# Gated attention plus gated FFN: gate ratios turned on TensorE, results finished block by block, spread factors on ScalarE's queue

## The chip, the cores and the metric

The kernel runs on one core of one Trainium2 chip. The metric is the device time of one execution in microseconds; the time before is the median of three runs. Smaller is better. All arithmetic is in float32; where a matmul needs the accuracy, a number is split into a high and a low part and three matmuls replace one.

## The reference

One sequence x of 2048 tokens with 640 features goes through two branches, and a gate per token mixes them:

```python
g = sigmoid((x * gate_w).sum(-1, keepdims=True))
a = attention(x, wq, wk, wv, wo, beta)   # 32 heads of 20, four chunks of 512 tokens
b = (silu(x @ w1) * (x @ w3)) @ w2       # 640 -> 1728 -> 640
out = g * a + (1 - g) * b
```

The attention works on chunks of 512 tokens. In each chunk a causal softmax attention inside the chunk is mixed, by a factor per head, with a read from a memory: `phi(q) @ M / phi(q) @ z`, where M and z are the sums over all earlier chunks of `phi(k)^T v` and `phi(k)`.

The kernel computes the result as `(1 - g) * (b + e * a)` with `e = g / (1 - g)`. The numbers `1 - g` and `e` per token are called here the gate's ratios. `e` is multiplied into the attention's own factors, so that the attention's projection can be added straight to the FFN's sums; `1 - g` scales each result at the very end.

## The kernel before

Everything is kept with features on the partitions and 512 tokens of a chunk along the row, so that a result block is 128 x 512 and a chunk has five (KB). Weights come from DRAM in tiles of 128 x 640 (`wr`, two raw buffers), are split by ScalarE (high part, L104) and GpSimd (low part, L105) into six buffers `W`, and are asked for ahead of their use by `w_step`, which counts steps of the program.

The four chunks are done in two pairs, A = (0, 1) and B = (2, 3). For each pair: projections v, k, q (`v_blocks` L341, `k_block` L380, `q_block` L304), then the FFN in five groups of inner blocks (`ffn_up` L465, `ffn_down` L500, whose sums live in a slot `acc` per chunk), the normalisation of the attention's result (`normalize` L684) and its projection by wo (`oproj` L761), which is added to the same `acc`. The attention runs in quads of four heads (32 quads): scores s (L567) for the row maxima (DVE, L574), the maxima turned and written beside the queries (mr, a DMA of ScalarE's queue, L588), scores again turned (t, L600), exponentials by ScalarE (P, L606), the causal cut by GpSimd (L610), and P times v (o, L620).

TensorE's order is written out by hand: the generator `attention` gives the attention's places, and `step` with a credit in nanoseconds puts the matmuls of the projections and the FFN between them; `braid(a, b, n, skip)` takes one place of job b after every n places of job a, from place `skip` on. The lists of jobs (L858 to L904) are the segments of the program. The orders of all other engines come from a scheduler with its own estimates of durations, except where `here` keeps an instruction at its place. Each engine executes its own list strictly in order, DMA issues included: a DMA that waits holds what is behind it on the issuing engine. DMAs are issued by SP (most), GpSimd (queries and keys of the attention, the weights for k, results of chunks 0 and 1) and ScalarE (mr, v and the gate's ratios).

The buffers that matter here: the tag `acc` has two slots, taken in turn by raw x, V, the FFN sums of a chunk and pq3; the tag `spread` has two buffers (rb and sh); eight PSUM banks go round by `bank_tile` (L109), each filled by TensorE and freed by the engine that reads it.

The pieces that the change touches:

- **Gate.** `v_blocks` gets the gate's sum as one more column of v, ScalarE takes its exponential per token block (L371), DVE makes the two ratios (L375 to L377) in `gate[:, c]`, tokens on the partitions, and L378 stores them to DRAM (`ed`) from there: 128 x 8 single elements, on ScalarE's queue, four steps later.
- **Factors.** When a chunk's quads are done, `o_sums` reads the softmax sums rs and the ratios er, `o_scale` (L656) forms one factor per head and token and writes it to DRAM spread over the 20 rows of a head (`rd`, four DMAs on SP, L661). `normalize` reads it back in five blocks of 128 rows (`rb`, SP, L693), two ahead; L694 and L695 issue the first two, `load(b + 2)` ahead of the yield the others. Each block multiplies `oall`, adds the transposed memory read for chunks 1 to 3 (gt, L706), and is split again.
- **Result.** `load_share` (L669) reads `1 - g` spread over 128 rows (`sh`, SP, L671). For chunks 2 and 3 the last `ffn_down` adds, multiplies (GpSimd for even blocks, DVE for odd) and stores on SP (L523 to L530). For chunks 0 and 1 a job `store(c)` (L789) does it later, braided into other work: five products on GpSimd (L794), five stores on GpSimd's queue (L795).

Of the kernel before, what the change touches and what calls it, by code (L numbers as in the profile page):

```python
# [38 lines left out]
def gated_mix(ctx: ExitStack, tc: tile.TileContext, xT, wqk, wv, w13, w2, w2h, wo, beta, out):  # L39
# [20 lines left out]
    cR = cp.tile([P, 1], F32, name="cR")  # L60
    rs = cp.tile([P, P], F32, name="rs")
    er = cp.tile([P, P], F32, name="er")
    nsT = [cp.tile([P, 32], FR, name=f"ns{i}") for i in range(2)]
    gate = cp.tile([P, NSEG, 2, 4], F32, name="gate")
    Ms = {}
# [275 lines left out]
    def v_blocks(c, iv, end):  # L341
        x = Xs[c]
        keep = c < NSEG - 1
        if keep:
            V = slot(f"V{c}").rearrange("p (l h e) -> p l h e", l=4, e=VE)
            big["v", c] = V
            nc.gpsimd.memset(V[:, :, :, DH:], 1.0)
        wvt = [w_get(i, iv[0]) for i in iv]
        for lb in range(4):
            if keep:  # L350
                vv = V[:, lb]
            else:
                vv = ht_tile([P, H, VE], F32, f"vv{c}_{lb}")
                nc.gpsimd.memset(vv[:, :, DH:], 1.0)
            for hf in range(2):
                n0, n1 = (0, 320) if hf == 0 else (320, 642)
                ps = bank_tile(f"v{c}_{lb}_{hf}", 800)
                n = 0
                for kb in range(KB):
                    for a, b in PASSES:  # L360
                        nc.tensor.matmul(ps[:, :n1 - n0], x[:, a, kb, lb * P:(lb + 1) * P],  # L361
                                         wvt[kb][:, b, n0:n1], start=n == 0, stop=n == 14)
                        n += 1
                    if end and (lb, hf) == (3, 1):
                        clock["oldest"] = iv[kb] + 1
                    if kb in (1, 3):
                        yield 890
                filled()
                last["act"] = nc.scalar.copy(vv[:, 16 * hf:16 * hf + 16, :DH], ps[:, :320].rearrange("p (h e) -> p h e", e=DH))
                if hf == 1:  # L370
                    nc.scalar.activation(gate[:, c, 1, lb:lb + 1], ps[:, 320:321], AF.Exp)  # L371
                yield 450
            store_later(vd[c][:, lb], vv.rearrange("p h e -> p (h e)"), ("v", c, lb), nc.scalar)
        e, g = gate[:, c, 1], gate[:, c, 0]
        nc.vector.tensor_scalar(e, e, TOP, None, op0=ALU.min)  # L375
        nc.vector.tensor_scalar(g, e, 1.0, None, op0=ALU.add)
        nc.vector.reciprocal(g, g)  # L377
        store_later(ed[c].rearrange("x a p -> p (x a)"), gate[:, c].rearrange("p x a -> p (x a)"), ("e", c), nc.scalar)  # L378

    def k_block(c, mb, i, prev):  # L380

        if prev:
            yield from memory_turn(*prev)
        ps = bank_tile(f"k{c}_{mb}", 1300)
        for n, y in enumerate(proj(ps, w_get(i), Xs[c])):
            yield y
            if n == 3 and prev:
                yield from memory_write(*prev)
        pk = None
        if c < NSEG - 1:  # L390
            big["k", c, mb] = pk = f_tile(f"pk{c}_{mb}")
        s = parts(f"ks{c}_{mb}", ps, pk)
        store_parts(1, c, mb, s)
        yield 699
# [102 lines left out]
                nc.vector.tensor_sub(ht[64:, 0], t[:64], ht[:64, 0].bitcast(F32))  # L497
            yield 699

    def ffn_down(cs, js, idx, last=False):  # L500
        first = js[0] == 0
        w2s = [w_get(i, idx[0]) for i in idx]
        for c in cs:
            if first:
                accs[c] = slot(f"acc{c}")[:, :KB * L].rearrange("p (b n) -> p b n", b=KB)
            if last:
                load_share(c)
            for fb in range(KB):
                ps = bank_tile(f"f{c}_{js[0]}_{fb}", 1300 if len(js) > 2 else 690)
                ms = []  # L510
                for j, w in zip(js, w2s):
                    for a, b in (PASSES if j < NF else ((0, 0), (0, 1))):
                        ms.append((w[:, b, fb * P:(fb + 1) * P], hts[c, j][:, a, :]))
                for n, (w, h) in enumerate(ms):
                    nc.tensor.matmul(ps, w, h, start=n == 0, stop=n == len(ms) - 1)  # L515
                    if n % 3 == 2 and n < len(ms) - 1:
                        yield 699.0 if n == 2 else 699
                filled()
                dst = accs[c][:, fb]
                if first:  # L520
                    nc.scalar.copy(dst, ps)  # L521
                elif not last:
                    nc.vector.tensor_add(dst, ps, dst)  # L523
                else:
                    end = (c, fb) == (cs[-1], KB - 1)
                    for n0 in ((0, 256) if end else (0,)):
                        d, p, g = (t[:, n0:n0 + (256 if end else L)] for t in (dst, ps, shares[c]))
                        nc.vector.tensor_add(d, p, d)
                        (nc.vector if end or fb % 2 else nc.gpsimd).tensor_mul(d, d, g)
                        nc.sync.dma_start(out[c, fb, :, n0:n0 + d.shape[-1]], d)  # L530
                yield 699 if len(ms) % 3 == 0 else 466

    oall, heads, pairs = {}, {}, {}
# [122 lines left out]
    def o_scale(c):  # L656

        here(nc.vector.reciprocal(rs, rs))
        nc.vector.scalar_tensor_tensor(rs, rs, cR, er, op0=ALU.mult, op1=ALU.mult)
        for a in range(4):  # L660
            here(nc.sync.dma_start(rd[c][:, :, a * P:(a + 1) * P], rs[a::4].unsqueeze(1).broadcast_to([H, DH, P])))  # L661
        turned.append(c)

    shares = {}
# [3 lines left out]

    def load_share(c):  # L669
        shares[c] = spread(f"sh{c}")  # L670
        here(nc.sync.dma_start(shares[c], ed[c][0].rearrange("a n -> (a n)").unsqueeze(0).broadcast_to([P, L])))  # L671

    gms = {}

# [9 lines left out]
    def normalize(c):  # L684

        rows = rd[c].rearrange("h e n -> (h e) n")
        rb = {}

        def load(b):
            if b < KB:  # L690
                assert c in turned
                rb[b] = spread(f"rb{c}_{b}")
                here(nc.sync.dma_start(rb[b], rows[b * P:(b + 1) * P]))  # L693

        load(0)  # L695
        load(1)
        yield 1
        if not c:
            gms[c] = big_tile(f"oT{c}", FR)[:, :KB * L].rearrange("p (b n) -> p b n", b=KB)
        for b in range(KB):  # L700
            o, hi = rb[b], gms[c][:, b]
            nc.vector.tensor_mul(o, oall[c][:, b].bitcast(F32), o)
            if c:
                pt = bank_tile(f"gt{c}_{b}")
                for qb in range(4):
                    nc.tensor.transpose(pt[:, qb * P:(qb + 1) * P], hi[:, qb * P:(qb + 1) * P].bitcast(F32), ident)  # L706
                nc.vector.tensor_add(o, o, pt)
            nc.scalar.copy(hi, o)
            nc.vector.tensor_sub(oall[c][:, b], o, hi.bitcast(F32))
            load(b + 2)  # L710
            yield 450 if c else 1

    NJ = NSEG * H

# [46 lines left out]
    def oproj(c, plan):  # L761
# [6 lines left out]

        def rest():
            ws.extend(w_get(i, plan[0]) for i in plan)  # L770
            for fb in range(KB):
                ps = bank_tile(f"op{c}_{fb}", 1300)
                n = 0
# [7 lines left out]
                        yield 699  # L781
                filled()
                dst = accs[c][:, fb]
                nc.vector.tensor_add(dst, ps, dst)
                yield 699

        return first(), rest()

    def store(c):  # L789
        load_share(c)  # L790
        yield 1
        for fb in range(KB):
            d = accs[c][:, fb]
            nc.gpsimd.tensor_mul(d, d, shares[c])  # L794
            here(nc.gpsimd.dma_start(out[c, fb], d))  # L795
            yield 1


    GROUPS = [[0, 1, 2], [3, 4, 5], [6, 7, 8], [9, 10, 11], [13, 12]]

# [5 lines left out]
        return [[((2 if j < NF else 1) * 3.5, ffn_up((c,), j, p, plans[0][0])) for j, p in zip(GROUPS[g], plans)]  # L806
                for c in cs]

    def job_down(cs, g, last=False):
        return 2.32 * sum(3 if j < NF else 2 for j in GROUPS[g]), ffn_down(cs, GROUPS[g], plan_down(GROUPS[g]), last)  # L810

    def jobs_up(cs, g):
# [62 lines left out]
    u0, u1 = jobs_up_by_chunk(A, 4)  # L875
    x2, x3 = split_x(2), split_x(3)
    seg += [(0, load_raw(2)), (0, load_raw(3))] + u0 + [braid(chain(u1), (0, x2), 4, 0, False)]
    d = job_down(A, 4)
    q = job_q(B[:1], 0, {2: big_tile})
    seg += [braid(chain([braid(braid(d, (0, store(0)), 2, 8), (0, x2), 5)] + q), (0, x3), 4, 10)] + job_v(B)  # L880
    kb_, turns, writes = jobs_k(B)
    seg += kb_ + turns[:1] + job_q(B[1:], 0, {3: slot}) + turns[1:] + writes
    segs.append((2 * H - 2, seg))
# [7 lines left out]
    segs.append((2 * H + LAG + 2, seg))  # L891
    up.append(job_up(B, 2))
    o1, o2 = jobs_oproj(1)
    seg = [braid(chain(up[1:]), o1, 4, 11), braid(o2, job_read(3), 3, 1), braid(job_down(B, 0), (0, store(1)), 3, 2), braid(chain(jobs_up(B, 1)), (0, load_memory(2)), 5)]
    segs.append((3 * H + LAG + 1, seg))
    d = job_down(B, 1)
    u = [job_up(B, j) for j in GROUPS[2][:2]]
# [3 lines left out]
    segs.append((NJ + LAG, seg))  # L901
    d, u = job_down(B, 3), jobs_up(B, 4)
    o1, o2 = jobs_oproj(3)
    tail = [braid(chain([d] + u), o1, 2, 8)] + [o2, job_down(B, 4, True)]  # L904

    for n, (_, g) in enumerate(head):
        for _ in g:
# [112 lines left out]
```

## Time and profile before

| | us |
|---|---|
| median of 3 runs | 1163.38 (1162.63 to 1166.82) |
| the profiled execution | 1161.55 |
| its span, first to last instruction | 1159.6 |
| TensorE busy (matmuls) | 1104.2 (95%) |
| DVE busy | 582.0 (50%) |
| GpSimd busy | 505.1 (44%) |
| ScalarE busy | 460.4 (40%) |
| mean granted clock of TensorE | 0.979 |

The trace gives each instruction with its start and length in microseconds from the span's start, its engine (PE is TensorE, PEld its weight loads, DVE VectorE, ACT ScalarE, POOL GpSimd, SP SyncE; a q behind the name is a DMA issue of that engine), the line of the kernel, the operation with output and input tiles, and in brackets the idle time of the engine just before and what ended it. A group of like instructions near each other is one row with a count (x15), whose length reaches from the first start to the last end. In the views by windows, each engine has its busy time and in brackets its instructions; then come the granted clock, the share of the 16 DMA engines' time that was busy (packets in flight overlap, so it can pass 1), and GB/s.

### The profile page before, as it was taken

Reading aid. Unit: us, or ns where it says so; the run is one execution under the profiler, and the core shown is the slowest. Engines: PE = TensorE matmul, PEld = TensorE weight load, DVE = VectorE, ACT = ScalarE, POOL = GpSimd, SP = SyncE. Lnnn points to the kernel's source line nnn. Section 1 sums busy time; section 2 is a strip of 40 time slices with the busy share of each in tenths; the row PEclk is TensorE's granted clock in tenths of the full one; section 3 lists DMA queues with packets and bytes.
Section 4 is the critical chain, followed back from the end, with each engine's and each line's share of the span. In section 5 each row is a group of like instructions: output and inputs, shape, how many; then the busy total and the mean of one; then the engine's idle time right before and its main releaser. Section 6 shows DMA issues by size and latency. Waiting matters only on the chain. (4 is left out here: it accounts for less than half of the span.)

```text
span 1159.6 us, 17915 instructions
## 1 busy us (share of the span) xinstructions
PE 1104.2 (95%) x6261; PEld 860.8 (74%) x6261; DVE 582.0 (50%) x1685; ACT 460.4 (40%) x948; POOL 505.1 (44%) x615
## 2 busy tenths in 40 slices
PE   9979999999999999998799997996999889999997
PEld 6968877777777777777677775774777667777785
DVE  5022474355555544474234675772556565561454
ACT  5245334444343324264345543442544343334130
POOL 4044445355354336264254444344654444454143
PEclk8989999999999999999999998998999999999999
DMA  8475853335354426326886868444565444432422
GB/s 300 97 151 209 275 145 90 90 84 131 78 137 122 124 72 181 106 70 195 93 261 205 295 189 202 109 126 120 150 156 146 108 101 107 116 105 85 127 75 99
DMA packets 102648, 163.28 MB, mean 141 GB/s; under 512 B 14560, under 2 KB 38368, under 8 KB 102560
## 3 DMA queue, kind: packets, MB, share of 16 engines
q1 hardware_dynamic: 73760, 114.81, 33.2%
q0 software_dynamic: 21184, 41.30, 15.9%
q10 hardware_dynamic: 7616, 6.05, 2.9%
q8 instruction: 49, 0.80, 0.3%
q14 instruction: 39, 0.32, 0.1%
HBM read 101.80 MB, written 59.79 MB: 139 GB/s over the span
## 5 line engine op out<-in xcount | busy, mean ns | idle before, releaser
L105 POOL TENSOR_TENSOR W<-wr,W 128x640 fp32r<-128x640 f32 (+1 forms) x126 | 197.2, 1571 | 298.1 <-ACT W L104 268.3
L574 DVE CUSTOM_DVE_ANT_0 junk<-s,mask 128x256 bf16<-128x256 f32 (+3 forms) x512 | 250.2, 489 | 118.2 <-PE s L567 85.7
L606 ACT ACTIVATE P<-t 128x512 f32<-128x512 f32 (+1 forms) x384 | 171.9, 536 | 143.6 <-PE t L600 117.0
L250 PE MATMUL g<-X,W 128*128 128x512 f32 x840 | 211.2, 401 | 4.3 <-DVE m L574 3.3
L515 PE MATMUL f<-ht,W 128*128 128x512 f32 x820 | 197.3, 398 | 0.0
L250 PE MATMUL u<-X,W 128*128 128x512 f32 x780 | 195.5, 398 | 0.4 <-DVE m L574 0.4
L250 PEld LDWEIGHTS g<-X,W 128*128 128x128 f32 x840 | 157.4, 190 | 42.0 <-DVE m L574 3.8
L515 PEld LDWEIGHTS f<-ht,W 128*128 128x128 f32 x820 | 153.4, 189 | 36.5
L610 POOL TENSOR_SCALAR_AFFINE_SELECT P<-P 128x256 f32<-128x256 f32 x192 | 93.8, 500 | 176.4 <-ACT P L606 175.8
L250 PEld LDWEIGHTS u<-X,W 128*128 128x128 f32 x780 | 144.1, 188 | 35.1 <-DVE m L574 0.6
L104 ACT CAST W<-wr 128x640 fp32r<-128x640 f32 (+1 forms) x133 | 95.7, 728 | 141.1 <-PE u L250 22.3
L105 POOL TENSOR_TENSOR ht<-ft,ht 128x512 fp32r<-128x512 f32 x52 | 67.3, 1294 | 101.7 <-ACT ht L104 98.6
L620 PE MATMUL o<-P,vg 128*32 128x512 f32 (+3 forms) x1024 | 79.4, 452 | 12.3 <-ACT acc L521 9.0
L544 POOL DMA_DIRECT2D qk<-qkd x128 | 83.1, 651 | 12.8 <-PE t L600 12.7
L250 PE MATMUL k<-X,W 128*128 128x512 f32 x300 | 78.6, 410 | 6.9 <-ACT P L606 6.9
L567 PE MATMUL s<-qk 60*128 60x256 f32 (+3 forms) x512 | 77.8, 346 | 4.0 <-DVE ft L489 1.7
L250 PE MATMUL q<-X,W 128*128 128x512 f32 x300 | 76.7, 410 | 1.5 <-ACT W L104 1.0
L361 PE MATMUL v<-W,X 128*128 128x320 f32 (+1 forms) x480 | 72.3, 311 | 4.1 <-POOL W L105 2.6
L361 PEld LDWEIGHTS v<-W,X 128*128 128x128 f32 x480 | 71.1, 189 | 5.1 <-POOL W L105 3.2
L620 PEld LDWEIGHTS o<-P,vg 128*32 128x32 f32 x1024 | 31.2, 113 | 56.5 <-issue 34.6
L523 DVE TENSOR_TENSOR acc<-f,acc 128x512 f32<-128x512 f32 x70 | 48.0, 689 | 47.5 <-PE f L515 47.4
L250 PEld LDWEIGHTS q<-X,W 128*128 128x128 f32 x300 | 57.3, 194 | 17.6 <-ACT W L104 1.5
(105 smaller groups left out, 1122.1 us busy)
## 6 DMA issues: line engine op xcount, KB each, us to landing
qk<-qkd POOLq DMA_DIRECT2D x128, 240.0 KB, 4.5
wr<-in_w_dram SPq DMA_DIRECT2D x80, 320.0 KB
qkd<-qs SPq DMA_DIRECT2D x20, 512.0 KB
qkd<-ks SPq DMA_DIRECT2D x20, 512.0 KB
od<-oq SPq DMA_DIRECT2D x32, 256.0 KB
wr<-in_wo_dram SPq DMA_DIRECT2D x20, 320.0 KB
vg<-vd SPq DMA_DIRECT2D x16, 336.0 KB
xr<-in_xT_dram SPq DMA_DIRECT2D x20, 256.0 KB
```

What stands on the lines that cost most here:

```text
L104: pin(nc.scalar.copy(dst[:, 0], src))
L105: (lo or nc.gpsimd.tensor_sub)(dst[:, 1], src, dst[:, 0].bitcast(F32))
L250: nc.tensor.matmul(ps, w[:, a, kb * P:(kb + 1) * P], x[:, b, kb, :], start=n == 0, stop=n == 14)
L361: nc.tensor.matmul(ps[:, :n1 - n0], x[:, a, kb, lb * P:(lb + 1) * P], wvt[kb][:, b, n0:n1], start=n == 0, stop=n == 14)
L515: nc.tensor.matmul(ps, w, h, start=n == 0, stop=n == len(ms) - 1)
L523: nc.vector.tensor_add(dst, ps, dst)
L544: here(nc.gpsimd.dma_start(t[64 * i:64 * i + RH], qkd[c][RH * (h + i):RH * (h + i + 1)]))
L567: nc.tensor.matmul(ps[i][:, o:o + w], q[:, qb * P:(qb + 1) * P], key[:, :w], start=n == 0, stop=n == len(todo) - 1, skip_group_check=True)
L574: nc.vector.tensor_tensor_reduce(out=junk[:, :w], in0=ps[i][:, o:o + w], in1=mask[:, L - w:], scale=1.0, scalar=-3.0e38, op0=ALU.add, op1= ...
L606: last["exp"] = nc.scalar.activation(pairs[2 * m + k]["P"][:, i, o:o + n], ps[i][:, b:b + n], AF.Exp, scale=SCALE)
L610: nc.gpsimd.affine_select(d, d, pattern=[[0, 2], [0, n], [1, P]], base=0, channel_multiplier=-1, compare_op=ALU.is_ge, fill=0.0)
L620: nc.tensor.matmul(ps[32 * i:32 * i + 32, kb * P:], heads[2 * p + i]["v"][:, kb], pairs[p + i // 2]["P"][:, i % 2, o:o + n], start=kb == 0 ...
```

## The change

Three things are done.

1. The ratios of a chunk are turned on TensorE: in the first k block of the chunk, after three of its yields (nine matmuls), `gate_turn` transposes `gate[:, c]` (128 x 8) to 8 x 128 in a PSUM bank, ScalarE copies it to one tile `et`, and SP stores it four steps later as eight rows of 512 bytes. The store of L378 goes.
2. `store(c)` and its two jobs go. A helper `finish` adds, multiplies and stores a block at its last sum, for all chunks: chunk 0 in the last `ffn_down` of pair A, chunk 1 in its projection, chunks 2 and 3 in the last `ffn_down` of pair B. Chunks 0 and 1 are stored on SP two steps later, chunks 2 and 3 at once.
3. The DMAs of rd, rb and sh are issued by ScalarE in place of SP, and `load(b + 2)` moves behind the yield of `normalize`.

With the jobs `store(0)` and `store(1)` their braids go too, so the splits of x for chunk 3 (x3) are woven into a shorter list of places; and in the tail the normalisation of chunk 3 is woven one place in five from the tenth on, where it was one in two from the eighth.

```diff
-        store_later(ed[c].rearrange("x a p -> p (x a)"), gate[:, c].rearrange("p x a -> p (x a)"), ("e", c), nc.scalar)
+
+    def gate_turn(c):
+        ps = bank_tile(f"ge{c}")
+        nc.tensor.transpose(ps[:8, :P], gate[:, c].rearrange("p x a -> p (x a)"), ident)
+        nc.scalar.copy(et, ps[:8, :P])
+        store_later(ed[c].rearrange("x a p -> (x a) p"), et, ("e", c))
...
         for n, y in enumerate(proj(ps, w_get(i), Xs[c])):
             yield y
+            if n == 2 and mb == 0:
+                gate_turn(c)
...
-    def ffn_down(cs, js, idx, last=False):
+    def finish(c, fb, ps, end=False):
+        dst = accs[c][:, fb]
+        for n0 in ((0, 256) if end else (0,)):
+            d, p, g = (t[:, n0:n0 + (256 if end else L)] for t in (dst, ps, shares[c]))
+            nc.vector.tensor_add(d, p, d)
+            (nc.vector if end or fb % 2 else nc.gpsimd).tensor_mul(d, d, g)
+            if c < 2:
+                store_later(out[c, fb], d, n=2)
+            else:
+                nc.sync.dma_start(out[c, fb, :, n0:n0 + d.shape[-1]], d)
+
+    def ffn_down(cs, js, idx, last=()):
...
         for c in cs:
+            if c in last:
+                load_share(c)
...
-            if last:
-                load_share(c)
...
-                elif not last:
+                elif c not in last:
                     nc.vector.tensor_add(dst, ps, dst)
                 else:
-                    end = (c, fb) == (cs[-1], KB - 1)
-                    for n0 in ((0, 256) if end else (0,)):
-                        d, p, g = (t[:, n0:n0 + (256 if end else L)] for t in (dst, ps, shares[c]))
-                        nc.vector.tensor_add(d, p, d)
-                        (nc.vector if end or fb % 2 else nc.gpsimd).tensor_mul(d, d, g)
-                        nc.sync.dma_start(out[c, fb, :, n0:n0 + d.shape[-1]], d)
+                    finish(c, fb, ps, (c, fb) == (NSEG - 1, KB - 1))
...
-            here(nc.sync.dma_start(rd[c][:, :, a * P:(a + 1) * P], rs[a::4].unsqueeze(1).broadcast_to([H, DH, P])))
+            here(nc.scalar.dma_start(rd[c][:, :, a * P:(a + 1) * P], rs[a::4].unsqueeze(1).broadcast_to([H, DH, P])))
...
-        here(nc.sync.dma_start(shares[c], ed[c][0].rearrange("a n -> (a n)").unsqueeze(0).broadcast_to([P, L])))
+        here(nc.scalar.dma_start(shares[c], ed[c][0].rearrange("a n -> (a n)").unsqueeze(0).broadcast_to([P, L])))
...
-                here(nc.sync.dma_start(rb[b], rows[b * P:(b + 1) * P]))
+                here(nc.scalar.dma_start(rb[b], rows[b * P:(b + 1) * P]))
...
-            load(b + 2)
             yield 450 if c else 1
+            load(b + 2)
...
         def rest():
             ws.extend(w_get(i, plan[0]) for i in plan)
+            if c == 1:
+                load_share(c)
...
-                nc.vector.tensor_add(dst, ps, dst)
+                if c == 1:
+                    finish(c, fb, ps)
+                else:
+                    nc.vector.tensor_add(dst, ps, dst)
                 yield 699
...
-    def store(c):
-        load_share(c)
-        yield 1
-        for fb in range(KB):
-            d = accs[c][:, fb]
-            nc.gpsimd.tensor_mul(d, d, shares[c])
-            here(nc.gpsimd.dma_start(out[c, fb], d))
-            yield 1
...
-    d = job_down(A, 4)
+    d = job_down(A, 4, (0,))
     q = job_q(B[:1], 0, {2: big_tile})
-    seg += [braid(chain([braid(braid(d, (0, store(0)), 2, 8), (0, x2), 5)] + q), (0, x3), 4, 10)] + job_v(B)
+    seg += [braid(chain([braid(d, (0, x2), 5)] + q), (0, x3), 4, 10)] + job_v(B)
...
-    seg = [braid(chain(up[1:]), o1, 4, 11), braid(o2, job_read(3), 3, 1), braid(job_down(B, 0), (0, store(1)), 3, 2), braid(chain(jobs_up(B, 1)), (0, load_memory(2)), 5)]
+    seg = [braid(chain(up[1:]), o1, 4, 11), braid(o2, job_read(3), 3, 1), job_down(B, 0), braid(chain(jobs_up(B, 1)), (0, load_memory(2)), 5)]
...
-    tail = [braid(chain([d] + u), o1, 2, 8)] + [o2, job_down(B, 4, True)]
+    tail = [braid(chain([d] + u), o1, 5, 10)] + [o2, job_down(B, 4, B)]
```

More of the change, by code (lines that the diff above doesn't have):

```diff
@@ L62, in gated_mix @@
     er = cp.tile([P, P], F32, name="er")
+    et = cp.tile([8, P], F32, name="et")
     nsT = [cp.tile([P, 32], FR, name=f"ns{i}") for i in range(2)]
@@ L709, in normalize @@
             nc.vector.tensor_sub(oall[c][:, b], o, hi.bitcast(F32))
+            yield 450 if c else 1
             load(b + 2)
-            yield 450 if c else 1
     NJ = NSEG * H
@@ L807, in jobs_up_by_chunk, with job_down @@
                 for c in cs]
-    def job_down(cs, g, last=False):
+    def job_down(cs, g, last=()):
         return 2.32 * sum(3 if j < NF else 2 for j in GROUPS[g]), ffn_down(cs, GROUPS[g], plan_down(GROUPS[g]), last)
```

## Prediction

> **What bounds the kernel now.** I read the table of engines first, then the table of TensorE's waits, then the time line around each long wait.
>
> ```profile
> PE   9979999999999999998799997996999889999997
> ```
> ```profile
> PE o L620 <- ACT acc L521: 9.0, 1, 9.0
> PE k L250 <- ACT P L606: 6.9, 1, 6.9
> PE pm L417 <- ACT pkn L404: 6.2, 1, 6.2
> ...
> PE v L361 <- POOL W L105: 2.6, 2, 1.4
> ```
>
> The first row gives TensorE's busy tenths in 40 slices of 29 us: nearly all are 9, so TensorE sets the time, and the end can move only where it waits, where its clock is low, or behind its last matmul. The second fence (releaser: us in total, times, longest) names the places. Its first three waits are 22 us together. The change leaves TensorE's own order as it is but for four small transposes and later turns in the tail, so I go from wait to wait and ask which of its three parts reaches it.
>
> **The change part by part.** The sum is made against the profiled execution: 1161.55 us, a span of 1159.6 and 1.95 around it, 1.8 below the median of 1163.38.
>
> **Part 1, the gate's ratios as rows.** Before, each store of the ratios is 128 x 8 elements of 4 bytes. Two of the four stand ahead of a stall.
>
> ```profile
> 62.34 1.09 POOL L161 DMA_DIRECT2D wr<-in_wqk_dram  x2
> 62.71 0.38 ACTq L269 DMA_DIRECT2D ed<-gate  x1
> 74.33 0.72 ACT L104 CAST W<-wr 128x640 fp32r<-128x640 f32 x1 [4.03 <-DMA wr<-in_wqk_dram]
> 76.56 2.33 PE L417 MATMUL pm<-V,pkn 128*128 128x147 f32 x8 [6.19 <-ACT pkn L404]
> 82.97 1.16 PE L417 MATMUL pm<-V,pkn 128*128 128x147 f32 x8
> ```
> ```profile
> DMA to landing us min/median/max: 3.3/5.2/11.4
> ```
> ```profile
> 550.00:560.00 10.00, 10.00 (x70) 10.00 (x69) 0.00 (x0) 2.28 (x7) 0.00 (x0) 1.00 0.84 68
> ```
> ```profile
> q1 hardware_dynamic: 73760, 114.81, 33.2%
> ```
>
> A time-line row is start, length, engine, line, operation, and in brackets the idle time and what ended it. Two weight loads (wr) and one ratio store (ed) leave together at 62.3 to 62.9. The second load is cast only at 74.33, 11.4 us after its issue, which is the longest landing of all weight loads where the median is 5.2. ScalarE stands in line at that cast, the copy pkn comes behind it, and TensorE waits 6.19 us. The window 550 to 560, where the third such store is in flight, has the DMA engines 84% taken at only 68 GB/s: many tiny pieces. That is 8.4 us of all 16 engines. SP's queue (q1) moved 114.81 MB in 33.2% of the span, 298 GB/s, so 0.68 MB are some 2.3 us of it, and I estimate 6 us for one ratio store. Without it I let the second load land 6.2 us after issue, one over the median: cast at 69.1 in place of 74.33, and the stall shrinks by 5.2. The eight pm matmuls took 2.33 in place of 1.16 at low clock, so 1.2 more: **6.4**. Bounds: 0 (the store was not the cause) and 6.19 + 1.2 = 7.4.
>
> The second place:
>
> ```profile
> 565.91 3.64 PE L250 MATMUL k<-X,W 128*128 128x512 f32 x15
> 568.19 1.15 POOL L161 DMA_DIRECT2D wr<-in_wqk_dram  x2
> 568.56 0.38 ACTq L269 DMA_DIRECT2D ed<-gate  x1
> 579.88 0.72 ACT L104 CAST W<-wr 128x640 fp32r<-128x640 f32 x1 [2.50 <-DMA wr<-in_wqk_dram]
> 581.16 5.35 PE L250 MATMUL k<-X,W 128*128 128x512 f32 x15 [6.94 <-ACT P L606]
> ```
>
> The same pattern: loads and store leave together, the second cast runs 11.1 us after issue, the attention's exponentials (P) stand behind it, and TensorE waits 6.94 us. With a landing 5.7 us after issue the cast runs at 574.5, k resumes near 576: 5.2 won, and 5.35 - 3.64 = 1.7 of low clock: **6.9**. Bounds 0 and 8.6.
>
> What part 1 adds: four transposes of 128 x 8 (0.15 us each, as the pm matmuls with 1.16 for eight), four ScalarE copies of one bank, and a wait of the second copy for the first store, since one tile holds both. **0.6** lost, bounds 0 and 3.
>
> **Part 2, results finished at their last sum.** The stall of 9.0 us:
>
> ```profile
> 773.13 0.69 DVE L784 TENSOR_TENSOR acc<-op,acc 128x512 f32<-128x512 f32 x1 [0.92 <-PE op L776]
> 800.23 2.77 POOL L795 DMA_DIRECT2D out_dram<-acc  x5
> 806.98 1.07 ACT L521 COPY acc<-f 128x512 f32<-128x512 f32 x2 [6.46 <-DMA out_dram<-acc]
> 807.62 4.50 PE L620 MATMUL o<-P,vg 128*32 128x512 f32 x32 [9.03 <-ACT acc L521]
> 706.43 2.36 PE L620 MATMUL o<-P,vg 128*32 128x512 f32 x32
> ```
> ```profile
> 784.02 0.59 ACT L521 COPY acc<-f 128x512 f32<-128x512 f32 x1 [1.76 <-PE f L515]
> ```
>
> The last sum of chunk 1 is there at 773.8, but its stores leave GpSimd only at 800 to 803, and the first copy of chunk 3's sums into the same slot waits for them; the PSUM bank behind it holds TensorE. After the change each block is multiplied and stored at its last sum: 773.8 + 1.3 + some 1.4 for two steps + 4.1, the longest landing of these stores, is about 780.6. In the changed order the first copy of chunk 2's sums is what waits for this slot, and it isn't due before 784.0: 3.4 us spare. The stall goes whole, and the 32 matmuls behind it fall from 4.50 to 2.36: 9.0 + 2.1 = **11.1**. What is late next is a store held in SP's queue; bounds 6 and 11.2.
>
> The tail:
>
> ```profile
> 1139.62 11.46 PE L515 MATMUL f<-ht,W 128*128 128x512 f32 x49
> 1148.24 0.43 SPq L671 DMA_DIRECT2D sh<-ed  x1
> 1151.98 2.36 DVE L529 TENSOR_TENSOR acc<-acc,sh 128x512 f32<-128x512 f32 x2 [1.34 <-DMA sh<-ed]
> 1154.94 1.15 DVE L529 TENSOR_TENSOR acc<-acc,sh 128x256 f32<-128x256 f32 x2
> ```
>
> The factors of chunk 3 (sh) leave at 1148.24, behind five stores in SP's queue, so its products start at 1152 and end at 1156.1, five us after the last matmul (1151.1). Issued from ScalarE they are there early; then only the additions and products of the last halves, of at most 0.58 each (1.15 for two), follow the last matmul, some 1.7 us with the overlap: 1152.8, **3.0** won (bounds 1.5 and 3.5).
>
> The place around 520, where part 2 costs:
>
> ```profile
> 523.25 1.56 POOL L105 TENSOR_TENSOR W<-wr,W 128x642 fp32r<-128x642 f32 x1
> 524.87 0.56 PE L361 MATMUL v<-W,X 128*128 128x320 f32 x2 [1.37 <-POOL W L105]
> 526.06 1.08 POOL L161 DMA_DIRECT2D wr<-in_wqk_dram  x2
> 528.07 0.37 POOL L347 MEMSET V<- 128x128 f32 x1 [0.36 <-DMA out_dram<-acc]
> 531.40 2.77 PE L361 MATMUL v<-W,X 128*128 128x322 f32 x17 [1.46 <-ACT P L606]
> ```
>
> GpSimd has two of five products and five stores less to issue here, which relieves the two v waits (2.6 together in the table). But in the changed order the fill of V2, which waits until all five stores of chunk 0 have landed (I estimate 519.5), stands ahead of the two W subtractions and of both weight loads on GpSimd: 519.5 + 0.4 + 2 x 1.56 = 523, then the loads. The splits of X3 come later too, since the job they are woven into gives fewer places, and attention matmuls wait for banks that these splits hold, behind the cast of that same load on ScalarE. The load lands 3.3 to 5.2 later, near 527. Then ScalarE has the cast (0.72), ten exponentials (3.7, by 2.19 for six in a row quoted below) and three splits (two passes of 0.6 each, as the copy of 0.59 above: 3.6), with hand-offs about 9 us: TensorE resumes the v block at 536 where it did at 531.4. With 1.4 of low clock (1.2 to 2.1 followed the three long waits) it is **6.0 lost**. Bounds: 3 won (the waits of this place go) and 9 lost.
>
> **Part 3, queues.** The spread factors (rd, rb, sh) leave SP, where they waited for free, and stand in line with ScalarE's work.
>
> ```profile
> SPq L693 <- DVE oall L709: 32.9, 10, 5.6
> ```
> ```profile
> 698.11 7.17 SPq L661 DMA_DIRECT2D rd<-rs  x4
> 709.31 2.19 ACT L606 ACTIVATE P<-t 128x512 f32<-128x512 f32 x6 [0.98 <-PE t L600]
> 718.87 4.21 PE L250 MATMUL g<-X,W 128*128 128x512 f32 x9 [3.33 <-DVE m L574]
> ```
> ```profile
> 1089.82 14.26 SPq L693 DMA_DIRECT2D rb<-rd  x5
> ```
> ```profile
> 1122.04 17.50 PE op L776 x75
> ```
>
> The four rd issues of chunk 1 filled 7.17 us of SP's queue: from 698.1 to 705.3, just ahead of the attention quad whose o matmuls run at 706.4. The loads of rb waited 32.9 us for the block before; the diff puts them behind a yield, so most of that wait should be over when ScalarE reaches them. I take **1.5 lost** over chunks 0 to 2. Bounds: 3 won (the 3.3 us wait at 718.9 stands behind late rb loads) and 10 lost (chunks 1 and 2 each 5, of a 7.17 us hold). In the tail the last rb left at 1104.1 and the projection starts at 1122.0, so chunk 3 has some 10 us to spare behind its last product, and costs nothing; that cover is gone if the loads come 10 us later.
>
> **Sum.** 1161.55 - 6.4 - 6.9 + 0.6 - 11.1 - 3.0 + 6.0 + 1.5 = 1142.25, so **1142**.
>
> **The rivals.**
> - *The ratio store isn't what delays the weights.* The Trainium skill, "DMA: Bandwidth & Descriptors", section "Queues, rings and completion order", says that each DMA engine takes turns between the queues at the grain of a packet; then tiny pieces of one queue would let the packets of another pass. In this kernel that means: 6 us for 1024 pieces is 64 pieces of 0.094 us on each engine; a load of 128 rows is 8 pieces per engine, each passed by one tiny piece: 0.75 us of delay, not 5. Then both stalls stay but for about 1.5 us together with their clock, 11.8 less is won: **1154**. For it: the large qkd stores of SP run there too. Against: the 11.4 us landing, and 84% at 68 GB/s.
> - *ScalarE is held (slower).* If the rd issues hold ScalarE as they held SP (7.17 us in chunk 1) and each rb wait (5.6 at the longest) stands there as well, exponentials and gm casts come late and TensorE's banks run out. It decides once a hold exceeds the 1 us that ScalarE idles between groups of exponentials there (0.98 at 709.31). Chunks 1 and 2 at 7.2 + 5.6 + 2.1 of clock is 30: **1172**. For it: this queue is in order, and every one of 40 issues has a wait that SP hid. Against: the yield ahead of rb, and that the rd hold ends before the quad.
> - *The stores of chunk 1 land late*, held in SP's queue behind weight loads, and the copy of chunk 2's sums waits in place of chunk 3's: the 11.1 us stay, **1153**. For it: only 3.4 us spare. Against: the other four blocks are summed, and leave, one by one before the last.
>
> **How the numbers follow.** The forecast has 0.55; the ratio-store rival 0.15, the held ScalarE 0.20, the late stores 0.10. The forecast's own range, the unknowns of 520 (-9 to +3) and of part 3 (-10 to +3) beside partial gains, is 1132 to 1152; it takes in the stores' rival up to a microsecond, and the range has to reach over the ratio-store rival with one further microsecond or two of loss: **1132 to 1160**; left out is most of the held ScalarE. A run of this kernel can tell 0.5%, that is 5.8 us, so faster is below 1155.7 and slower above 1167.4. Faster: 0.55 + 0.10 + 0.10 of the ratio-store rival + 0.02 of weak holds = 0.77; same 0.05 + 0.06 = 0.11; slower 0.12.
>
> **What would show it.** Right: no TensorE wait for pkn near 71 to 76 and none of 7 us near 575, with weight casts there about 6 us after issue; windows with a store of ratios at far below 0.84 of DMA share for their bytes; no wait for acc at 800; the last product within 2 us of the last matmul. A new wait of 4 to 6 us between 525 and 536, behind an X3 split or an exponential. Wrong: weight casts 11 us after issue still (first rival); ScalarE rows that idle before an rd or rb issue while TensorE waits for P (second); a wait of TensorE for L521's copies near 784 (third). My weakest terms are those of 520 and of part 3, whose new waits no row of before shows.

## The result, and the profile after

The changed kernel takes **1131.72 us** (median of 4, 1128.63 to 1133.71), the one before 1165.1 in the runs beside it; the ratio is **0.971 (95%: 0.967 to 0.975)**, 33 us. The forecast was 1142 with a range from 1132, so the gain was named but too small by 10 us, and the time lies 0.3 us below the range. The profiled execution took 1131.51 us, its span is 1129.7.

TensorE has the same matmuls in the same order in both kernels, but for four transposes and chunk 3's turns. So each matmul of one trace can be paired with itself in the other, and the difference of the two starts, followed along the time, tells where time was won or lost. Where that difference moved:

| stretch of the trace before, us | forecast | traces |
|---|---|---|
| first 15 us (q projection, granted clock) | 0 | -1.6 |
| first k blocks, 60 to 85 | -6.4 | -7.5 |
| around 520 (v blocks of the second pair) | +6.0 | +5.6 |
| k block of chunk 3, 575 to 590 | -6.9 | -7.6 |
| normalisation of chunk 1, 680 to 765 | +1.5 for chunks 0 to 2 together | -0.7 |
| around 780 (granted clock) | 0 | -1.3 |
| accumulator's copy, 800 to 885 | -11.1 | -11.6 |
| normalisation of chunk 2, 885 to 1000 | (in the +1.5) | -2.3 |
| behind the last matmul | -3.0 | -2.9 |
| four transposes and copies | +0.6 | in the rows above |
| sum | -19.3 | -29.9 |

Two rows can't be laid to the change. The first 15 us were 0.3 to 3.1 us shorter in the traces of all other kernels here than in this one trace of before, with an unchanged program; the granted clock was 0.77 in it and 0.89 in the trace of the changed kernel. Around 780 the clock was 0.74 for 5 us before and 1.00 after, and in the traces of the kernels below that have neither part 2 nor part 3 this place moved by -2.2 to +2.0. TensorE's waits after the change (releaser: us in total, times, longest):

```profile
PE t L614 <- DVE X L131: 5.7, 3, 3.9
PE gt L720 <- DVE m L588: 4.3, 2, 2.7
PE t L614 <- DVE m L588: 2.7, 2, 1.9
PE g L251 <- DVE m L588: 1.4, 1, 1.4
```

The three long waits are gone; the longest is now the new one for X near 520. The time line at the first k blocks, and the landings of the weight loads. The trace gives a landing only for the ten loads that GpSimd issues, so the 11.4 of the prediction too is the longest of these ten:

```profile
60.71 1.10 POOL L162 DMA_DIRECT2D wr<-in_wqk_dram  x2
61.10 0.34 SPq L270 DMA_DIRECT2D ed<-et  x1
64.88 0.72 ACT L105 CAST W<-wr 128x640 fp32r<-128x640 f32 x1
68.81 1.16 PE L425 MATMUL pm<-V,pkn 128*128 128x147 f32 x8
```
```profile
DMA to landing us min/median/max: 3.2/4.0/6.1
```

The second weight tile is cast 3.6 us after its issue in place of 11.4, no cast waits, pm follows without a wait and at full clock. The longest of the ten landings fell from 11.4 to 6.1. At the k block of chunk 3:

```profile
564.65 1.15 POOL L162 DMA_DIRECT2D wr<-in_wqk_dram  x2
569.57 1.40 ACT L105 CAST W<-wr 128x640 fp32r<-128x640 f32 x2
571.51 2.36 PE L251 MATMUL k<-X,W 128*128 128x512 f32 x9 [0.69 <-ACT P L620]
```

Both casts run together and the wait of 6.94 is 0.69. At the accumulator's copies and in the tail:

```profile
763.47 0.34 SPq L270 DMA_DIRECT2D out_dram<-acc  x1
771.29 0.58 ACT L540 COPY acc<-f 128x512 f32<-128x512 f32 x1
785.46 2.36 PE L634 MATMUL o<-P,vg 128*32 128x512 f32 x32
```
```profile
1109.85 0.81 ACTq L685 DMA_DIRECT2D sh<-ed  x2
1112.38 11.70 PE L534 MATMUL f<-ht,W 128*128 128x512 f32 x50
1125.73 0.74 DVE L513 TENSOR_TENSOR acc<-acc,sh 128x256 f32<-128x256 f32 x2
```

The last store of chunk 1 leaves at 763.5, the first copy into its slot runs at 771.3, the 32 o matmuls take 2.36 and wait for nothing. In the tail sh is asked for 16 us early and the last product ends 2.4 us after the last matmul (1124.1), where it was 5.

### The profile page after: what moved, and what is told of

The parts are those of the page before. It is cut to its first block, busy times and chain, and to the rows that moved or that the text cites. A ratio compares the mean times of both kernels' runs of the same rounds, so it can differ in the third digit from the quotient of the medians.

```text
span 1129.7 us, 17927 instructions
## 1 busy us (share of the span) xinstructions
PE 1099.9 (97%) x6265; PEld 856.5 (76%) x6265; DVE 584.8 (52%) x1689; ACT 460.0 (41%) x952; POOL 494.5 (44%) x601
## 3 DMA queue, kind: packets, MB, share of 16 engines
q1 hardware_dynamic: 61312, 105.91, 29.9%
## 4 chain that ended last, share of the span: by engine, by line
PE 83%; DMA 4%; issue 4%; DVE 3%; POOL 3%; ACT 2%; SPq 0%; ACTq 0%; DVEq 0%; POOLq 0%
PE g L251 16%; PE f L534 15%; PE u L251 15%; PE k L251 6%; PE v L362 6%; PE q L251 6%; PE o L634 5%; PE s L581 4%; PE op L792 4%; PE t L614 3%; DMA rb<-rd 2%; PE pm L425 1%; PE nd L329 1%; POOL W L106 1%; ACT P L620 1%
## 5 line engine op out<-in xcount | busy, mean ns | idle before, releaser
L614 PE MATMUL t<-qk 62*128 62x256 f32 (+3 forms) x512 | 65.0, 324 | 9.8 <-DVE X L131 5.7
L542 DVE TENSOR_TENSOR acc<-f,acc 128x512 f32<-128x512 f32 x65 | 44.4, 689 | 49.0 <-PE f L534 48.9
```

Source lines behind the costliest of these rows:

```text
L614: nc.tensor.matmul(ps[i][:, o:o + L - kb * P], key[:, kb * P:(kb + 1) * P], q[:, kb * P:], start=n == 0, stop=n == len(todo) - 1, skip_gro ...
```

## The experiments

Aligned by TensorE's instructions as above, "trace" below is the sum of such differences; ratios are timed, against the kernel before.

### The three parts, each alone, and parts 2 and 3 together

The edit of `e1_gate_rows` is part 1 of the diff on the kernel before, `e2_blocks` part 2 with its changed braids and all factors still issued by SP, `e3_factors_act` part 3:

```diff
 e1  -store_later(ed[c] ..., gate[:, c] as 128 x 8, ("e", c), nc.scalar)
     +gate_turn(c) after nine matmuls of the first k block
 e2  -store(0), store(1)
     +finish(c, fb, ps) at each last sum
 e3  -nc.sync.dma_start(rd / rb / sh)     +nc.scalar.dma_start(rd / rb / sh)
     -load(b + 2) ahead of the yield      +load(b + 2) behind it
 e4  the changed kernel, with e1's edit undone
```

> The kernel before with part 1 alone (ratios turned on TensorE, eight rows of 512 bytes, stored by SP). Aligned by TensorE's instructions, the changed kernel gained 8 us in the first k blocks and 7 us at the k block of the second pair. Theory (tiny pieces hold up the weight loads): both come with part 1 alone, 13 to 16 us faster, and the waits for pkn (6.2) and for P ahead of k (6.9) are gone. Rival (the tiny pieces are passed by, the gain is from elsewhere): within 3 us of before, both waits still there.

> The kernel before with part 2 alone (results finished block by block at the last sum), factors still on SP. Theory: the wait of 9 us for the accumulator's copy goes with its low clock, 12 us won; the place around the v blocks of the second pair loses about 6; the tail's wait for sh stays, as sh is still behind SP's stores. Net 4 to 8 us faster. Rival (the 12 us need sh or the factors off SP): the wait at the accumulator moves to chunk 2's copy and 3 us or less are won, or the kernel is slower.

> The kernel before with part 3 alone (rd, rb and sh on ScalarE's queue, load behind the yield). Theory formed from the two traces: rb no longer stands behind weight loads in SP's queue and mr no longer shares the engines with rd, so chunk 1 wins 2, chunk 2 wins 3 and the tail 3: 6 to 9 us faster. Rival (my prediction's own step): 1 to 2 us lost in the normalisations, 3 won in the tail, 1 to 2 us faster. Second rival (ScalarE is held): slower.

> The changed kernel without part 1: the ratios are stored as 4-byte elements by ScalarE as before. Theory: 13 to 16 us slower than the changed kernel, so 1145 to 1149, with the waits for pkn and for P ahead of k back. Rival (ratio store not the cause): within 3 us of the changed kernel.

| | median us | ratio (95%) |
|---|---|---|
| part 1 alone | 1142.61 | 0.981 (0.978 to 0.983) |
| part 2 alone | 1153.94 | 0.990 (0.987 to 0.994) |
| part 3 alone | 1157.77 | 0.994 (0.992 to 0.996) |
| parts 2 and 3 | 1148.71 | 0.986 (0.985 to 0.988) |
| all three | 1131.72 | 0.971 (0.967 to 0.975) |

Part 1 brings both waits down by itself: it is worth 19 to 26 us alone by the clock of the timed runs, 14.5 in the trace beside the first 15 us, and 17 when it is the last to be added. The rival that the ratio store isn't the cause is out. Part 2 wins some 11.5 us at the accumulator's copy with sh on SP and loses 4.3 near 520; parts 1 to 3 alone add up to 3.6%, together they give 2.9%. Part 3 alone wins 5 to 9 us in the timed runs. In its trace 3.3 are won in the tail and 4.7 in chunk 2, but chunk 1, where I had read a gain, is 0.3 longer; the whole trace is only 3.5 shorter than before's, as the two stalls behind the ratio stores, which part 3 leaves alone, came out 3.4 longer in it.

### Is it ScalarE's queue or the tiny pieces?

```diff
 e5  -store_later(ed[c] ..., ("e", c), nc.scalar)   +store_later(ed[c] ..., ("e", c))
 e6  +store_later(ed[c] ..., None, nc.scalar)       a second time, into the same tile
 e7  +store_later(ex[c] ..., None, nc.scalar)       a second time, into a tile of its own
```

> The kernel before, with the same 4-byte store of the ratios issued by SP in place of ScalarE. Theory (the tiny pieces take the DMA engines, whoever issues them): the waits of TensorE for pkn (6.2) and for P ahead of k (6.9) stay within 2 us, the weight casts there still run over 9 us after their issue. Rival (ScalarE's queue or the issue in ScalarE's line is what delays its casts): both waits fall below 2 us and the time to 1148 or less.

> The kernel before, with every 4-byte store of the ratios issued twice (the same data once more). Theory: each store is some 6 us of all DMA engines, so each of the two waits grows by 4 to 7 us: pkn to 10 to 13, P ahead of k to 11 to 14, the time to 1170 to 1178. Rival (taking turns by packet, tiny pieces pass others by at 0.75 us a load): each wait grows by under 1.5 us and the time stays below 1168.

> The kernel before, with every 4-byte store of the ratios followed by a second one of the same data into a DRAM tile of its own, so that the second doesn't wait for the first as it did in the run with the store issued twice. Theory (tiny pieces take the DMA engines): the two waits of TensorE ahead of pm and of k grow by 4 to 8 us each and the span by 9 to 18 with their clock. Rival (pieces of one queue let the others pass): each wait grows by under 1.5 us.

Waits of TensorE with the 4-byte store on SP's queue, then with two stores on ScalarE's:

```profile
PE k L250 <- ACT P L606: 8.2, 1, 8.2
PE pm L417 <- ACT pkn L404: 7.3, 1, 7.3
```
```profile
PE pm L419 <- ACT pkn L406: 8.5, 2, 7.1
PE k L251 <- ACT P L608: 8.4, 1, 8.4
```

On SP's queue (1160.01 us, before 1160.24) both waits stay: it is the pieces, not who issues them. The run with the store twice into one tile took 1187.83 us, but not for the reason that I meant to test:

```profile
59.65 15.14 ACTq L269 DMA_DIRECT2D ed<-gate  x2
```

Its second store, into the same tile, waits on ScalarE until the first has landed. In the four pairs of that run the second issue stands 10.7 to 16.0 us behind the first, so the run tells only that one such store of 4 KB needs over 10 us to land. With a tile of its own (1164.87 us) the waits are 2.3 and 1.5 us above the kernel before, against 4 to 8 expected; the longest two, 7.1 and 8.4, are about as long as the 7.3 and 8.2 with a single store on SP's queue, so the second store costs TensorE nothing that these runs can tell. So my price, 6 us of the DMA engines in proportion to the pieces, is wrong though the cause is right.

### What the stall goes by

Four runs put a further store, which nobody reads, beside part 1's rows.

```diff
 h1  +ex[c] = [2, 4, 128]        1024 pieces of 4 bytes, neighbouring tokens in neighbouring words
 h2  +ex[c] = [2, 4, 128, 128]   1024 pieces of 4 bytes, each 512 bytes from the next
 h3  +ex[c] = [2, 4, 128]        half of h1: 512 pieces
 h4  +ex[c] = [128, 8]           the same 4 KB as 128 pieces of 32 bytes
```

> Part 1 alone (rows), and beside it the old 4-byte store as a further one into a DRAM tile that nobody reads: 1024 pieces, neighbouring tokens in neighbouring words. Both theories: the waits ahead of pm and of k come back, 5 to 9 us each.

> The same further store of 1024 pieces of 4 bytes, but each piece 512 bytes from the next in DRAM. Theory C (the cost goes by the number of pieces): waits as with the dense store, 5 to 9 us each. Theory L (neighbouring words written by 16 engines get in each other's way in memory): both waits under 1.5 us.

> The same further store with half the pieces (512 of 4 bytes, dense). Theory C: each wait is half or less of the dense store's, 1 to 4 us. A fixed cost per such store: as the dense one, 5 to 9.

> The same further store with the same 4 KB as 128 pieces of 32 bytes, each token's eight ratios side by side. Theory C: an eighth, each wait under 1.5 us. Theory L: two to sixteen pieces still share a stretch of memory, 1 to 5 us.

Times of one run each: 1162.18, **1138.44**, 1161.06, 1144.05 us (part 1 alone 1142.61). Waits with the dense store, then with half of it:

```profile
PE k L252 <- ACT P L616: 8.1, 1, 8.1
...
PE pm L427 <- ACT pkn L414: 6.7, 1, 6.7
```
```profile
PE k L252 <- ACT P L616: 7.1, 1, 7.1
PE pm L427 <- ACT pkn L414: 5.6, 1, 5.6
```

With spread pieces and with pieces of 32 bytes the wait for pkn is gone, and that for P ahead of k is 0.9 and 0.7. The DMA view of 58 to 78 us, GB/s in slices of half a microsecond, dense pieces first, then spread ones:

```profile
GB/s 0 151 398 140 0 102 246 277 162 283 174 31 35 18 25 74 59 41 57 41 49 45 37 29 45 74 160 225 307 324 20 1 29 385 381 230 162 210 326 356
```
```profile
GB/s 0 242 392 54 0 154 307 198 244 366 373 399 397 383 75 45 1 274 385 287 215 123 328 371 412 377 113 0 0 356 389 339 108 97 352 372 216 32 67 333
```

After dense pieces all transfers of the core crawl at 18 to 74 GB/s from 63.5 to 71 us; after the same number of pieces spread over memory they run at 200 to 400 for most of it. The packet records of the two traces say when. The 1024 pieces themselves take 9 ns each in both and have all started by 62.7. What follows differs: from 63.5 to 71, packets of 512 bytes and more take 721 ns in the mean with dense pieces (146 of them, 0.33 MB) and 103 ns with spread ones (933, 2.04 MB). So it isn't the number of pieces alone and not the engines' time for them: it is that 4-byte pieces of different partitions fall close together in memory. Half the pieces, as densely packed, cost nearly as much, which speaks against a price in proportion to their number. The 128 pieces of 32 bytes cost nothing that TensorE sees, where I had expected 1 to 5 us by place and under 1.5 by number; as both the size and the number differ there, this run can't tell which it is. What distance between 4 and 512 bytes is enough wasn't tried. The Trainium skill, "DMA: Bandwidth & Descriptors", section "Specifications", says that a transfer below 512 B is done as read-modify-write. The pieces of all four stores are below that, and two of the stores bring no stall, so this alone isn't the cause; that such cycles line up when they meet in one stretch of memory would fit, but no run here shows what happens inside the memory. In the run with two stores in two tiles the crawl takes in the second store as well: its pieces, 9 ns each before the crawl, take 60 to 253 ns in the mean of each microsecond from 63 to 69.

### rd and rb, one at a time

```diff
 e8_rd_sp  the changed kernel, -nc.scalar.dma_start(rd ...)  +nc.sync.dma_start(rd ...)
 e9_rb_sp  the changed kernel, -nc.scalar.dma_start(rb ...)  +nc.sync.dma_start(rb ...), load(b + 2) ahead of the yield
```

> The changed kernel with rd alone back on SP. Theory (mr is no longer overtaken by rd when rd stands behind it on one queue): the wait of t for mr, 3.1 before and absent after, comes back, 2 to 4 us slower than the changed kernel, chunk 2 unchanged. Rival (rd's queue is without effect; rb is what matters): within 1.5 us of it.

> The changed kernel with rb alone back on SP, its load ahead of the yield again. Theory (rb behind weight loads in SP's queue comes late): the wait of o for POOL P in chunk 2 (3.25, with 1.7 of low clock) comes back, 3 to 6 us slower than the changed kernel, chunk 1 within 2. Rival (ScalarE's queue holds its casts, so taking rb off it wins): 1 to 4 us faster.

With rb back on SP: 1135.21 us, ratio 0.979 (0.975 to 0.983), on the same chip as 1129.73 (0.972, 0.969 to 0.975) with rd back. Chunk 2 in the kernel before, in the changed one, and with rb on SP again:

```profile
909.29 6.10 SPq L161 DMA_DIRECT2D wr<-in_wo_dram  x3
915.49 0.86 SPq L693 DMA_DIRECT2D rb<-rd  x2
...
921.66 0.67 DVE L707 TENSOR_TENSOR rb<-rb,gt 128x512 f32<-128x512 f32 x1
...
922.48 4.06 PE L620 MATMUL o<-P,vg 128*32 128x512 f32 x32 [3.25 <-POOL P L610]
```
```profile
887.77 0.90 ACTq L707 DMA_DIRECT2D rb<-rd  x2
...
893.22 0.67 DVE L721 TENSOR_TENSOR rb<-rb,gt 128x512 f32<-128x512 f32 x1
...
894.46 2.36 PE L634 MATMUL o<-P,vg 128*32 128x512 f32 x32
```
```profile
885.66 5.62 SPq L162 DMA_DIRECT2D wr<-in_wo_dram  x3
891.38 1.06 SPq L707 DMA_DIRECT2D rb<-rd  x2
...
898.02 0.67 DVE L721 TENSOR_TENSOR rb<-rb,gt 128x512 f32<-128x512 f32 x1
...
898.84 4.50 PE L634 MATMUL o<-P,vg 128*32 128x512 f32 x32 [3.25 <-POOL P L624]
```

These rows are the first two loads of rb, which the place of `load(b + 2)` doesn't move. On SP, rb stands behind three weight loads that wait for buffers, some 3 us later than on ScalarE. The turned memory read gt keeps its PSUM bank until DVE has added it to rb's product (L707, L721), and that addition is what the o matmuls wait for, since they get this bank next: the semaphores on which TensorE stands there are DVE's and its own, and the addition ends at 922.33 and o starts at 922.48, with rb on SP again at 898.69 and 898.84. The releaser in the bracket, GpSimd's cut of P, only happens to end last there; the P that these matmuls read were ready long before. In the changed kernel the addition ends at 893.89, ahead of the matmuls' turn. Behind the wait of 3.25 the 32 matmuls run at little over half pace. Together that is some 5 us at this place, and it goes with rb's queue: in the traces of all seven kernels with rb on ScalarE 5.1 to 5.6 us are won here against the kernel before, and in the ten with rb on SP no more than 0.5 either way. Not all of it stays won, as the section on the prediction shows; over the whole trace rb on SP costs some 3.5 beside the first 15 us, in the timed runs 5.5 against the run with rd back. With rd back, one row returns:

```profile
695.14 0.92 PE L614 MATMUL t<-qk 62*128 62x512 f32 x6 [2.87 <-DMA qk<-mr]
```

It costs 2.4 us in the trace, which the timed runs can't tell from nothing. It is no proof that rd's queue alone does it: with part 3 alone the same wait is still 2.9, though rd stands behind mr there too. What else it takes stays open.

### The place near 520

```diff
 f2  -braid(..., (0, x3), 4, 10)   +braid(..., (0, x3), 3, 5)
 f4  -braid(..., (0, x3), 4, 10)   +braid(..., (0, x3), 3, 3)
 g1  -w_add(wqk[KB + mb], D, nc.gpsimd)   +w_add(wqk[KB + mb], D, nc.sync if cs[0] else nc.gpsimd)
```

> The changed kernel with the splits of x for chunk 3 woven in at every third place from the fifth on (was every fourth from the tenth). Theory (the 6 us lost near 520 come from these splits standing behind a weight cast on ScalarE while attention's banks wait for them): with three splits done ahead, the wait of t for X (5.7 in all) falls to 1 to 3, 3 to 5 us faster than the changed kernel. Rival (the late weight load is what counts, the wait moves to P): within 1.5 us.

> The changed kernel with these splits at every third place from the third on: all five stand ahead of the weight cast. Theory: the wait of t for X is gone or under 1, 4 to 7 us faster than the changed kernel. Rival (late weight load): the cast still holds the exponentials behind it, a wait for P of 3 to 5 takes its place, within 2 us.

> The changed kernel with the weights of the second pair's k blocks loaded by SP in place of GpSimd, the splits as they are. Theory (order of the splits): the wait for X stays above 4, within 2 us of the changed kernel. Rival (the load's late issue behind GpSimd's fill of V2 and its subtractions): the cast comes 2 to 3 us earlier, the wait falls by as much, 2 to 4 us faster.

The changed kernel there, then the one with the splits earliest:

```profile
512.06 1.17 POOL L162 DMA_DIRECT2D wr<-in_wqk_dram  x2
516.85 0.72 ACT L105 CAST W<-wr 128x640 fp32r<-128x640 f32 x1 [2.21 <-DMA wr<-in_wqk_dram]
519.34 0.68 PE L614 MATMUL t<-qk 62*128 62x384 f32 x1 [3.93 <-DVE X L131]
522.02 4.49 PE L634 MATMUL o<-P,vg 128*32 128x512 f32 x32 [0.37 <-DVE X L131]
527.87 7.37 PE L362 MATMUL v<-W,X 128*128 128x322 f32 x48
```
```profile
515.24 2.36 PE L634 MATMUL o<-P,vg 128*32 128x512 f32 x32
516.05 0.73 ACT L105 CAST W<-wr 128x640 fp32r<-128x640 f32 x1 [0.35 <-DMA wr<-in_wqk_dram]
518.84 3.38 PE L362 MATMUL v<-W,X 128*128 128x322 f32 x21
```

The splits ahead of the cast bring the place 9 us forward, for **1122.12 us, ratio 0.965 (0.961 to 0.968)**, the best here; the middle setting gives 1124.23 (0.967, 0.964 to 0.970). Both are more than I expected. It is the order on ScalarE: the weight tile is cast at nearly the same time in both rows, but the splits no longer stand behind it. With the weights on SP the cast comes 3.1 us earlier (513.7) and the wait for X falls by 3.0, from 5.7 to 2.7, as the rival said; but 1.9 us are lost just ahead, in a wait for DVE's phi of the queries, and the time can't be told from the changed kernel's (1128.4, 0.970, 0.967 to 0.973). So the late load lengthens the wait, and the order makes it.

## Why the prediction was right and wrong

- **Right: where the time lay.** The three long waits, the tail and the new loss near 520 are the five largest steps in the table, and each came out within 1.1 us of its term in the trace.
- **Wrong: the sign of part 3.** "I take 1.5 lost over chunks 0 to 2" is the step that failed; 3.0 were won over chunks 1 and 2, and these 4.5 are the largest piece of the 10.6 that are missing. I priced what ScalarE would lose by the rd and rb issues, and of SP's side only the one wait in chunk 1, as a bound. In chunk 2 the wait of 3.2 named GpSimd's P, I took it at its name and left it out of the working; it was a bank that late rb products held, as the rows of chunk 2 above show. Some 5.5 us are won there. In this trace 3.2 of them are lost again behind it (0.4 to 3.2 in the seven traces with rb on ScalarE), as DVE stands for the next rb with the row maxima behind it:

```profile
904.70 0.69 DVE L716 TENSOR_TENSOR rb<-oall,rb 128x512 f32<-128x512 f32 x1 [3.96 <-DMA rb<-rd]
906.74 0.44 PE L614 MATMUL t<-qk 62*128 62x384 f32 x2 [1.89 <-DVE m L588]
```

- **Chunk 1 is no gain that the runs can tell.** The wait of t for mr, 3.1 before, was left out of the working too; it is gone, and 0.8 for DVE's maxima stand in its place. But the wait of 3.3 for DVE's row maxima, which the prediction held for a possible gain, didn't shrink: it is 1.4 at its old place and 2.7 at a new one just ahead, 4.1 together. Its named releaser is right; the maxima stand in DVE's line behind rb's product, for which DVE had waited 1.36 us before and waits 2.98 now. The first row is of the kernel before, the others of the changed one:

```profile
705.77 0.73 PE L600 MATMUL t<-qk 62*128 62x512 f32 x6 [3.14 <-DMA qk<-mr]
```
```profile
702.61 0.73 DVE L716 TENSOR_TENSOR rb<-oall,rb 128x512 f32<-128x512 f32 x1 [2.98 <-DMA rb<-rd]
...
703.60 0.66 PE L720 MATMUL gt<-ident,gm 128*128 128x128 f32 x4 [2.72 <-DVE m L588]
```

  On balance 0.7 was won from 680 to 765; in the traces of the kernels without part 3 the same stretch moved by -3.4 to +1.1.
- **ScalarE held: it happened and cost little.** The four rd issues of chunk 1 did hold ScalarE:

```profile
686.21 6.03 ACTq L675 DMA_DIRECT2D rd<-rs  x4
692.34 0.62 ACT L105 CAST ht<-ft 128x512 fp32r<-128x512 f32 x1 [7.31 <-DMA rd<-rs]
692.62 0.73 PE L614 MATMUL t<-qk 62*128 62x512 f32 x6 [0.83 <-DVE m L588]
```

  ScalarE stood 7.3 us until 692.3, 0.3 ahead of the quad. The slower rival's price was real, its condition wasn't met: nothing that TensorE needed soon was behind.
- **Right cause, wrong price: the ratio store.** The forecast's 6.4 and 6.9 were taken from the landings of the weights and held to 1.1 and 0.7; the 6 us "for one ratio store", 0.094 us for each piece on its engine, were a story about piece counts that the dose and the spread pieces deny. The pieces took 9 ns each, and the busy share of 84% was that of other packets made slow. In that window of 550 to 560 all pieces have started by 554, and from then to 559 the other packets of ScalarE's queue take 0.5 to 3.7 us in the mean of each microsecond. The rival that tiny pieces let others pass was wrong on the time (both waits go with the rows), but right that the pieces themselves take little of the engines.
- **Mis-sized: the landings.** In both k blocks 6.2 us of wait went where I had taken 5.2, since the second weight tile landed 3.5 and 4.9 us after its issue in place of 6.2 and 5.7. At the copy the wait came out as forecast, and the low clock behind it 0.4 longer. The 0.6 for the transposes shows nowhere. With 520 and the tail these sizes make 3.2 of the 10.6.
- **The range, and chance.** Part 3 came out at its bound of 3 won, which the range had in view. The other 2.9, from the first 15 us and the clock near 780, can't be laid to the change; without them the profiled execution would stand at some 1134, an estimate from the table above, inside the range. So that the time fell 0.3 us below it is chance, but the wrong sign of part 3 is not.

## What to carry to other kernels

Look at where small stores fall in DRAM, not only at how many pieces they have: a store of single words from many partitions into neighbouring words slowed every transfer of the core for about 8 us, and turning the block on TensorE first cost a transpose of 0.27 us and a copy of 0.25 us per chunk. Before moving DMAs off a queue, list for every one of them what stood ahead of it there and follow the waits of all engines back to it, not only the bottleneck's one releaser. And read a gain of a few microseconds from several traces: one stretch of 85 us moved by up to 3.4 us here between kernels in which it is the same. When a change removes places in a hand-woven order, look at what is woven by counting them: here a shift of a few places was worth 9 us, more than part 3 alone.

## What was not expected of the hardware

- A store of 1024 pieces of 4 bytes, side by side in memory, needs over 10 us to land and holds all transfers of the core at 18 to 74 GB/s for about 8 us, though its pieces take 9 ns each and the crawl begins when they are through; the same pieces 512 bytes apart, or 128 pieces of 32 bytes, don't hold the others up.
- A second such store at the same time into another tile lengthened TensorE's waits by nothing that could be told: 7.1 and 8.4 us at the longest, where one store in another run gave 7.3 and 8.2.
